# Whole-tile transposes of q and k, and a full-height last matmul, in an attention and feed-forward kernel

## Chip, cores, metric

One core of one Trainium2 chip. The metric is the device time of one execution in microseconds, lower is better.

## What is computed

Three layers one after another on 4 batches of 576 tokens: attention with 8 heads of 64 in a sliding window of 64 tokens, a convolutional gated feed-forward layer, and a second feed-forward layer with a product over the token axis.

```
scores = q @ k.T / 8, kept where 0 <= i - j < 64
x = softmax(scores) @ v                     # per head, then heads side by side: (4, 576, 512)
h = relu(x @ w_in)                          # 1024 wide
c = conv over tokens, 3 taps per channel
y = (h * sigmoid(c)) @ w_out
u, v = split(relu(y @ w2_in)); v = layernorm(v)
v_s = einsum('ts,bsd->btd', w_spatial, v) + b_spatial
out = (u * v_s) @ w2_out
```

The weights w_in, w_out, w2_in and w2_out arrive as 64-bit numbers and are turned into 32-bit ones on the chip.

## The kernel before

Large products run in a reduced 32-bit form on TensorE, with every operand split into a high part and the rest; high x high, high x rest and rest x high are summed in PSUM (`split`, line 288).

Nothing is written out in program order. Each operation is recorded with a rank (a due time), the engines that may run it with an estimated cost for each, and what it reads and writes (`Plan.op`, line 94); `Plan.emit` (line 115) then plays the estimates through and emits, on each engine, the ready operation of the lowest rank. The engines run what is emitted strictly in that order. So a changed cost in an operation can change the order of others. All loads are issued from one queue, SyncE's (SPq in the profile).

*Attention.* Batch 0 has its q and k loaded in five tiles of 128 tokens (the last has 64), by `rec_load_qk` (line 425), and transposed on TensorE by `rec_qk` (line 466): q goes into the block-diagonal tiles qbd, k into kT, by copies out of the PSUM tile tr, of which there is one. In tile 0 the tokens lie on 128 partitions, and four transposes of 128x128 do it (line 478). In tiles 1 to 4, chosen by `pairs` (line 422), two neighbouring tokens share a partition, so that 64 partitions (32 in the last tile) hold rows of 128 numbers; 16 small operations follow, 8 transposes (line 489) and 8 matmuls with the identity (line 487), and the copies put even and odd tokens back in place. The matmuls execute twice each for 32-bit operands, the transposes once. The other batches are transposed on VectorE.

A block of 64 queries is a round (`rec_round`, line 534): scores on TensorE (s, line 543), mask and row maximum on VectorE (line 555), exponential on ScalarE (line 563), reciprocal on VectorE (lines 570, 571), normalising on GpSimd or VectorE (line 575), transposes (pt, line 585), a copy to pts, the product with v (pv, line 598), and the split into x. There are 36 rounds. The PSUM tiles s, pt and pv exist once each.

*First feed-forward.* h (lines 681 to 683) starts when the first five rounds of batch 0 are through and the first slice of w_in is converted. A conversion takes two bit operations and a join on VectorE (lines 387, 393, 399) and a scaled copy on ScalarE, VectorE or GpSimd; its raw load goes into one of two raw tiles. The three taps of the convolution are VectorE work (line 709).

*Second feed-forward.* `rec_sp` (line 1003) computes the product over tokens for one batch, 128 channels and half of the tokens: 14 matmuls into one PSUM tile of 288 columns. The contraction runs over four whole tiles of 128 tokens, three matmuls each (lines 1018 to 1020), and over the last 64 tokens. For these, the tile vtl holds the high part of v on partitions 0 to 63 and the rest on 64 to 127, and the last tile of the spatial weights wspg holds its 64 rows twice. One matmul on 128 rows with the weights' high part gives two of the products (line 1023), one on 64 rows with the weights' rest gives the third:

```
mm(sps(), vv[:, ds], ws[:, 0, o], start=False, stop=False)
mm(sps(), vv[0:TAIL, ds], ws[0:TAIL, 1, o], start=False, stop=True)
```

There are 32 such groups, eight a batch. Behind each follow an add of the bias on VectorE (line 1032), a product with u on GpSimd or VectorE (line 1035), and the split into gd (lines 265 and 286); two gr tiles and two PSUM tiles take turns.

Of the kernel before, what the change touches and what calls it, by code (L numbers as in the profile page):

```python
# [19 lines left out]
# leads, spacings and engine weights of the plan below  # L20
# [45 lines left out]
class Buf:  # L66
    """One tile of a rotating tag, made when its first user is emitted."""
# [14 lines left out]
class Plan:  # L82
    """Orders the emission: each operation has a rank, engines it may run on with estimated
    costs, and the regions and tiles it touches. Recorded in an order that is right when run
    one after another; each engine then takes the ready operation of the lowest rank."""
# [105 lines left out]
def tile_attention_convglu_spatial(  # L191
# [59 lines left out]
    def mk(pool, shape, dt, tag, name, n):  # L251
        """A tile of a tag; `pool` may be a list that holds the pool when the tile is made."""
        return plan.buf(
            tag, n,
            lambda: (pool[0] if isinstance(pool, list) else pool).tile(shape, dt, tag=tag, name=name, bufs=n),
        )
# [31 lines left out]
    def split(rank, n, src, hi, lo, r, w, b, psum=False, hi_engs="AV", lo_engs="V", hi_cost=None):  # L288
        """hi = src to float32r; lo = src - hi, exact."""
        costs = {"A": c_act(n, psum), "V": c_tt(n) if psum else c_ts(n), "P": 0.00238 * n + 0.1}  # L290
        op(rank, {e: costs[e] for e in hi_engs}, lambda e: copy_to(e, hi(), src()), r=r, w=[(w, "h")], b=b)
        lc = {"V": c_tt(n), "P": 0.00238 * n + 0.1}
        op(
            rank + 0.01, {e: lc[e] for e in lo_engs}, lambda e: sub_to(e, lo(), src(), hi()),
            r=list(r) + [(w, "h")], w=[(w, "l")], b=b,
        )
# [84 lines left out]
    def halves(x_):  # L381
        """The 16-bit halves of 32-bit words, the low one first."""
        return x_.bitcast(H16).rearrange("p (c w) -> p c w", w=2)

    def low_bits(u, raw):
        """The upper three bits of the low words, as the lowest bits of u."""
        nc.vector.tensor_scalar(
            out=halves(u)[:, :, 0], in0=halves(raw.rearrange("p c w -> p (c w)"))[:, 0::2, 1],
            scalar1=13, scalar2=None, op0=ALU.logical_shift_right,
        )  # L390
# [31 lines left out]
    def pairs(t):  # L422
        return 30 >> t & 1

    def rec_load_qk(b, t, rank):
        """Batch 0: rows of tokens. Later: tokens in rows of 32, each group of 32 partitions
        with its 32 columns of a head pair."""
        for src, dst, nm in ((q, qn, "qn"), (k, kn, "kn")):
            if b < B0:
                n = min(P, S - t * P)  # L430
                if pairs(t):
                    a = mk(at, [W, H, 2 * D], F, nm, nm, 2)
                else:
                    a = mk(at, [P, H, D], F, nm, nm, 2)

                def ld(e, a=a, src=src, n=n):
                    if pairs(t):
                        nc.sync.dma_start(
                            out=a()[:n // 2], in_=src[b, :, t * P:t * P + n, :].rearrange("h (p r) d -> p h (r d)", r=2)
                        )  # L440
                    else:
                        nc.sync.dma_start(out=a()[:n], in_=src[b, :, t * P:t * P + n, :].rearrange("h p d -> p h d"))
                op(rank, {"D": (0.73 if pairs(t) else 1.46) * n / P}, ld, w=[(nm, b, t)], b=[a])
            else:
                a = mk(at, [P, HP, 2 * UB, 32], F, nm, nm, 2)
                n = UB * W
                for g in range(4):
                    def ld(e, a=a, src=src, g=g):
                        for hp in range(HP):
                            part = src[b, 2 * hp + g // 2, t * n:(t + 1) * n, 32 * (g % 2):32 * (g % 2) + 32]  # L450
                            nc.sync.dma_start(
                                out=a()[32 * g:32 * g + 32, hp], in_=part.rearrange("(u t) c -> t u c", t=32)
                            )
                    op(rank + 0.01 * g, {"D": 1.9}, ld, w=[(nm, b, t, g)], b=[a])
            dst[b, t] = a
# [10 lines left out]
    def rec_qk(b, t, rank):  # L466
# [3 lines left out]
        for nm, src in (("q", qn), ("k", kn)):  # L470
            a = src[b, t]
            two = pairs(t)
            pt_ = ps("y" if (b, t, nm) == (0, 0, "k") else "tr", [P, HP, 2, W] if two else [P, HP, P], "tr")

            def tr(e, a=a, pt_=pt_):
                for hp in range(HP):
                    if not two:
                        nc.tensor.transpose(
                            pt_()[:, hp, :n], a()[:n, 2 * hp:2 * hp + 2, :].rearrange("p h d -> p (h d)"), ident[:n, :n]
                        )  # L480
                        continue
                    for h in range(2):
                        for r_ in range(2):
                            o_ = pt_()[h * W:h * W + W, hp, r_, :n // 2]
                            i_ = a()[:n // 2, 2 * hp + h, r_ * D:r_ * D + D]
                            if h:
                                mm(o_, i_, ident[:n // 2, :n // 2], start=True, stop=True)
                            else:
                                nc.tensor.transpose(o_, i_, ident[:n // 2, :n // 2])

            def put(e, dst, rows, c0, m, pt_=pt_):
                if two:
                    copy_to(
                        e, dst.rearrange("p k (c r) -> p k r c", r=2), pt_()[rows, :, :, c0 // 2:(c0 + m) // 2]
                    )
                else:
                    copy_to(e, dst, pt_()[rows, :, c0:c0 + m])
            key = (nm, "tr", b, t)
            op(rank, {"T": HP * (0.32 if two else 0.112)}, tr, r=[(nm + "n", b, t), "ident"], w=[key], b=[a, pt_])
# [111 lines left out]
    def rec_conv(rank, src, view, n, dst=None, b=(), lead=PLAN["LD"]):  # L611
        """float64 words to float32; returns the tile and the key."""
# [164 lines left out]
    # the rounds, in order  # L777
# [186 lines left out]
    # transposed spatial weights: tiles of s on partitions; the last one holds its rows twice  # L964
# [38 lines left out]
    def rec_sp(b, d, c, rank):  # L1003
# [9 lines left out]
        def g(e):  # L1013
            for s in range(NT):
# [6 lines left out]
                else:  # L1021
                    vv = vtl[pp][bj]()
                    mm(sps(), vv[:, ds], ws[:, 0, o], start=False, stop=False)
                    mm(sps(), vv[0:TAIL, ds], ws[0:TAIL, 1, o], start=False, stop=True)  # L1024
# [139 lines left out]
```

## Time and profile before

| | |
|---|---|
| runs (3) | 584.22 us median, 584.21 to 586.52 |
| span of the profiled execution | 582.7 us, 11237 instructions |
| TensorE (PE) busy | 552.4 us, 95%, 4070 matmuls |
| VectorE (DVE) busy | 379.5 us, 65% |
| ScalarE (ACT) busy | 304.3 us, 52% |
| GpSimd (POOL) busy | 177.5 us, 30% |
| mean granted clock of TensorE | 0.967 |
| moved by DMA | 49.71 MB, mean 85 GB/s |

The span runs from the first to the last instruction; a run's time holds some 1.5 us more. A mean busy share hides that stages have different limits, so the views are read stage by stage. In the profile's rows L12 is line 12 of the kernel; the granted clock is a share of 2.4 GHz; PEld is the load of the stationary operand, which overlaps PE; the end of a matmul is modelled, so the distance between two starts says more than the duration of one.

### The profile page before, as it was taken

To read this page: it belongs to the slowest core of one execution; us is meant where nothing else is said; L and a number is where in the kernel's file an instruction comes from. 1 tells how busy PE (TensorE), PEld (TensorE's weight loads), DVE (VectorE), ACT (ScalarE), POOL (GpSimd) and SP (SyncE) were. 2 spreads that over 40 slices of the span, in tenths; PEclk is the share of its full clock that TensorE was granted. 3 is DMA by queue.
4 is the path that set the end of the run, shared out by engine and by line. 5 is a ranking of instruction groups with operands and counts; after the bars stand their busy time and mean duration, and the time that the engine had idled before them with its cause. 6 is when DMAs were issued, how large, how long until landed. Compare 5 with 4: busy or idle time off the path is not lost.

```text
span 582.7 us, 11237 instructions
## 1 busy us (share of the span) xinstructions
PE 552.4 (95%) x4070; PEld 504.0 (86%) x4070; DVE 379.5 (65%) x1021; ACT 304.3 (52%) x829; POOL 177.5 (30%) x163
## 2 busy tenths in 40 slices
PE   7999768899999999999999669999999999999997
PEld 6779657899999999999999669898898889888986
DVE  3469999876978587577559991997515661562050
ACT  4557645876866776677675642662322332233222
POOL 2547563440432423223325360024113100310130
PEclk9569989999999999999999888999999999999999
DMA  9647354345244344353136733320012011001002
GB/s 194 169 127 187 102 139 91 64 93 111 53 96 98 66 98 87 59 105 75 39 109 206 217 100 130 80 100 1 37 38 81 1 54 37 1 1 73 1 1 90
DMA packets 119418, 49.71 MB, mean 85 GB/s; under 512 B 99820, under 2 KB 111876, under 8 KB 119364
## 3 DMA queue, kind: packets, MB, share of 16 engines
q1 hardware_dynamic: 119364, 49.01, 33.4%
q8 instruction: 32, 0.52, 0.4%
q14 instruction: 22, 0.18, 0.1%
HBM read 39.54 MB, written 9.44 MB: 84 GB/s over the span
## 4 chain that ended last, share of the span: by engine, by line
PE 76%; DVE 16%; DMA 4%; ACT 2%; issue 2%; POOL 0%; SPq 0%; DVEq 0%; POOLq 0%; ACTq 0%
PE s L543 5%; DVE cv L709 5%; PE y L749 4%; PE y L748 4%; PE y L750 4%; PE sps L1018 4%; PE h L681 4%; PE h L682 3%; PE h L683 3%; PE vps L893 3%; PE sps L1020 3%; PE sps L1019 3%; PE ops L1071 3%; PE vps L894 3%; PE ops L1072 3%; PE vps L895 3%
## 5 line engine op out<-in xcount | busy, mean ns | idle before, releaser
L709 DVE SCALAR_TENSOR_TENSOR cv<-hs,cw,cv 128x288 f32<-128x288 f32 x128 | 86.5, 687 | 24.1 <-ACT cv L704 22.9
L681 PE MATMUL h<-x,wi 128*128 128x290 f32 x256 | 79.9, 312 | 11.1 <-ACT hs L281 8.3
L748 PE MATMUL y<-g,wo 128*128 128x288 f32 x256 | 80.7, 315 | 5.0 <-ACT g L265 2.8
L750 PE MATMUL y<-g,wo 128*128 128x288 f32 x256 | 77.4, 302 | 0.8 <-POOL wo L286 0.8
L749 PE MATMUL y<-g,wo 128*128 128x288 f32 x256 | 77.8, 304 | 0.2 <-DVE g L286 0.2
L682 PE MATMUL h<-x,wi 128*128 128x290 f32 x256 | 76.8, 300 | 0.5 <-DVE x L286 0.5
L683 PE MATMUL h<-x,wi 128*128 128x290 f32 x256 | 76.6, 299 | 0.0
L286 POOL TENSOR_TENSOR g<-cv,g 128x576 fp32r<-128x576 f32 x31 | 47.0, 1517 | 80.9 <-ACT g L265 79.4
L575 POOL TENSOR_TENSOR sm<-sm,st 128x512 f32<-128x512 f32 x36 | 39.5, 1098 | 71.2 <-DVE st L571 46.9
L681 PEld LDWEIGHTS h<-x,wi 128*128 128x128 f32 x256 | 49.1, 192 | 12.9 <-ACT hs L281 9.6
L563 ACT ACTIVATE sm<-sm,st 128x128 f32<-128x128 f32 x144 | 55.9, 390 | 8.1 <-DVE st L555 8.0
L748 PEld LDWEIGHTS y<-g,wo 128*128 128x128 f32 x256 | 49.9, 195 | 6.4 <-ACT g L265 3.0
L750 PEld LDWEIGHTS y<-g,wo 128*128 128x128 f32 x256 | 49.8, 195 | 1.1 <-POOL wo L286 1.1
L749 PEld LDWEIGHTS y<-g,wo 128*128 128x128 f32 x256 | 50.1, 196 | 0.5 <-DVE g L286 0.5
L682 PEld LDWEIGHTS h<-x,wi 128*128 128x128 f32 x256 | 49.2, 192 | 0.7 <-DVE x L286 0.7
L683 PEld LDWEIGHTS h<-x,wi 128*128 128x128 f32 x256 | 49.2, 192 | 0.0
L1035 POOL TENSOR_TENSOR gr<-gr,ut 128x288 f32<-128x288 f32 x30 | 25.4, 847 | 77.5 <-DVE gr L1032 74.7
L543 PE MATMUL s<-kT,qbd 128*128 128x128 f32 x288 | 42.8, 295 | 1.7 <-DVE kT L522 1.2
L1032 DVE TENSOR_TENSOR gr<-sps,bb 128x288 f32<-128x288 f32 x32 | 14.6, 456 | 44.9 <-PE sps L1024 44.8
L265 ACT ACTIVATE gd<-gr 128x288 fp32r<-128x288 f32 (+1 forms) x32 | 13.4, 417 | 56.3 <-POOL gr L1035 51.4
L555 DVE CUSTOM_DVE_ANT_0 sm<-s,mask_n 128x128 f32<-128x128 f32 x128 | 29.4, 285 | 19.2 <-PE s L543 19.1
L543 PEld LDWEIGHTS s<-kT,qbd 128*128 128x128 f32 x288 | 37.8, 203 | 3.6 <-DVE kT L522 1.6
(176 smaller groups left out, 1452.0 us busy)
## 6 DMA issues: line engine op xcount, KB each, us to landing
raw<-in_moe_w_in_dram SPq DMA_DIRECT2D x16, 512.0 KB, 4.9
vw<-in_v_dram SPq DMA_DIRECT2D x32, 256.0 KB, 3.8
raw<-in_moe_w_out_dram SPq DMA_DIRECT2D x12, 512.0 KB, 3.6
yd<-ys SPq DMA_DIRECT2D x32, 144.0 KB, 1.8
yr<-yd SPq DMA_DIRECT2D x16, 288.0 KB, 4.0
out_dram<-osb SPq DMA_DIRECT2D x15, 256.0 KB, 2.0
qn<-in_q_dram SPq DMA_DIRECT2D x144, 24.0 KB, 2.0
kn<-in_k_dram SPq DMA_DIRECT2D x144, 24.0 KB, 2.0
```

What stands on the lines that cost most here:

```text
L286: (nc.gpsimd if e == "P" else nc.vector).tensor_tensor(out=out_, in0=a, in1=b.bitcast(F), op=ALU.subtract)
L543: mm(pss()[:, hp, :], qbd[j][:, hp, :], kT[:, hp, k0 * W:k0 * W + P], start=True, stop=True,)
L555: nc.vector.tensor_tensor_reduce(out=sm()[:, hp, :], in0=pss()[:, hp, :], in1=mask, scale=-scale, scalar=BIG, op0=ALU.add, op1=ALU.min, ac ...
L563: nc.scalar.activation(out=sm()[:, hp, :], in_=sm()[:, hp, :], func=ACTF.Exp, scale=-1.0, bias=st()[:, 0, hp:hp + 1], accum_out=st()[:, 1, ...
L575: (nc.gpsimd if e == "P" else nc.vector).tensor_tensor(out=sm(), in0=sm(), in1=st()[:, 2, :].unsqueeze(2).to_broadcast([P, HP, P]), op=ALU ...
L681: mm(hps(), wh, xh, start=(kk == 0), stop=False)
L682: mm(hps(), wh, xl, start=False, stop=False)
L683: mm(hps(), wl, xh, start=False, stop=(kk == KD - 1))
L709: return lambda e: nc.vector.scalar_tensor_tensor(out=cv(), in0=h[:, o + j:o + j + CH], scalar=cw[:, j, f:f + 1], in1=cv(), op0=ALU.mult, ...
L748: mm(yps(), wt[:, 0], gt[:, 0, :], start=(kk == 0), stop=False)
L749: mm(yps(), wt[:, 0], gt[:, 1, :], start=False, stop=False)
L750: mm(yps(), wt[:, 1], gt[:, 0, :], start=False, stop=(kk == KF - 1))
```

## The change

Batch 0's tiles 1 to 4 of q and k are loaded and transposed as tile 0 is. The planner is told of longer loads (1.46 instead of 0.73 for 128 tokens) and shorter transposes (4 x 0.112 instead of 4 x 0.32). In the product over tokens the last matmul uses all 128 rows of vtl and of the weights' rest, which adds rest x rest, a product that was left out before. Comments are dropped too.

```diff
-    def pairs(t):
-        return 30 >> t & 1
...
                 n = min(P, S - t * P)
-                if pairs(t):
-                    a = mk(at, [W, H, 2 * D], F, nm, nm, 2)
-                else:
-                    a = mk(at, [P, H, D], F, nm, nm, 2)
+                a = mk(at, [P, H, D], F, nm, nm, 2)
 
                 def ld(e, a=a, src=src, n=n):
-                    if pairs(t):
-                        nc.sync.dma_start(
-                            out=a()[:n // 2], in_=src[b, :, t * P:t * P + n, :].rearrange("h (p r) d -> p h (r d)", r=2)
-                        )
-                    else:
-                        nc.sync.dma_start(out=a()[:n], in_=src[b, :, t * P:t * P + n, :].rearrange("h p d -> p h d"))
-                op(rank, {"D": (0.73 if pairs(t) else 1.46) * n / P}, ld, w=[(nm, b, t)], b=[a])
+                    nc.sync.dma_start(out=a()[:n], in_=src[b, :, t * P:t * P + n, :].rearrange("h p d -> p h d"))
+                op(rank, {"D": 1.46 * n / P}, ld, w=[(nm, b, t)], b=[a])
...
                 for hp in range(HP):
-                    if not two:
-                        nc.tensor.transpose(
-                            pt_()[:, hp, :n], a()[:n, 2 * hp:2 * hp + 2, :].rearrange("p h d -> p (h d)"), ident[:n, :n]
-                        )
-                        continue
-                    for h in range(2):
-                        for r_ in range(2):
-                            o_ = pt_()[h * W:h * W + W, hp, r_, :n // 2]
-                            i_ = a()[:n // 2, 2 * hp + h, r_ * D:r_ * D + D]
-                            if h:
-                                mm(o_, i_, ident[:n // 2, :n // 2], start=True, stop=True)
-                            else:
-                                nc.tensor.transpose(o_, i_, ident[:n // 2, :n // 2])
+                    nc.tensor.transpose(
+                        pt_()[:, hp, :n], a()[:n, 2 * hp:2 * hp + 2, :].rearrange("p h d -> p (h d)"), ident[:n, :n]
+                    )
 
             def put(e, dst, rows, c0, m, pt_=pt_):
-                if two:
-                    copy_to(
-                        e, dst.rearrange("p k (c r) -> p k r c", r=2), pt_()[rows, :, :, c0 // 2:(c0 + m) // 2]
-                    )
-                else:
-                    copy_to(e, dst, pt_()[rows, :, c0:c0 + m])
+                copy_to(e, dst, pt_()[rows, :, c0:c0 + m])
...
-            op(rank, {"T": HP * (0.32 if two else 0.112)}, tr, r=[(nm + "n", b, t), "ident"], w=[key], b=[a, pt_])
+            op(rank, {"T": HP * 0.112}, tr, r=[(nm + "n", b, t), "ident"], w=[key], b=[a, pt_])
...
                     mm(sps(), vv[:, ds], ws[:, 0, o], start=False, stop=False)
-                    mm(sps(), vv[0:TAIL, ds], ws[0:TAIL, 1, o], start=False, stop=True)
+                    mm(sps(), vv[:, ds], ws[:, 1, o], start=False, stop=True)
```

TensorE's order at the head of the program, before the change (tr is the PSUM tile of the transposes, qn and kn the loaded tiles of q and k, s the scores; the two rows of small operations come four times in a set):

```order
L478 MATMUL tr<-ident,qn 128x128 x4
L478 MATMUL tr<-ident,kn 128x128 x4
L489 MATMUL tr<-ident,qn 64x64 x2
L487 MATMUL tr<-ident,qn 64x64 x2
...
L543 MATMUL s<-kT,qbd_90 128x128 x4
L413 MATMUL cwp<-ident,cwf 128x24
L489 MATMUL tr<-ident,kn 64x64 x2
L487 MATMUL tr<-ident,kn 64x64 x2
...
L543 MATMUL s<-kT,qbd_91 128x128 x4
```

And with the change (lines are those of the changed kernel):

```order
L465 MATMUL tr<-ident,qn 128x128 x4
L465 MATMUL tr<-ident,kn 128x128 x4
L516 MATMUL s<-kT,qbd_90 128x128 x4
L465 MATMUL tr<-ident,qn 128x128 x4
L413 MATMUL cwp<-ident,cwf 128x24
L516 MATMUL s<-kT,qbd_91 128x128 x4
L465 MATMUL tr<-ident,kn 128x128 x4
L516 MATMUL s<-kT,qbd_92 128x128 x4
```

The scores of the first block now stand ahead of the transposes of tile 1 of q, and those of the second ahead of tile 1 of k.

SyncE's loads from the third load of w_in on (raw), before:

```order
L619 DMA raw<-in_moe_w_in_dram 128x4x256
L438 DMA qn<-in_q_dram 64x8x128
L438 DMA kn<-in_k_dram 64x8x128
L619 DMA raw<-in_moe_w_in_dram 128x4x256
L438 DMA qn<-in_q_dram 32x8x128
L438 DMA kn<-in_k_dram 32x8x128
```

And with the change:

```order
L592 DMA raw<-in_moe_w_in_dram 128x4x256
L431 DMA qn<-in_q_dram 128x8x64
L431 DMA kn<-in_k_dram 128x8x64
L451 DMA vw<-in_v_dram 128x8x64
L592 DMA raw<-in_moe_w_in_dram 128x4x256
L451 DMA vw<-in_v_dram 128x8x64
L592 DMA raw<-in_moe_w_in_dram 128x4x256
L431 DMA qn<-in_q_dram 64x8x64
L431 DMA kn<-in_k_dram 64x8x64
```

Two loads of v and the fifth of w_in now stand ahead of the last tile of q and k; a load of v stands ahead of the fourth of w_in.

## Rows read from the trace of the kernel before

**Rows 1.** Stretches: us, busy us of PE, PEld, DVE, ACT, POOL, then clock, DMA, GB/s

```profile
0.00:8.00 8.00, 5.57 (x32) 5.33 (x32) 2.73 (x9) 2.88 (x6) 2.50 (x21) 1.00 0.74 160
...
16.00:39.00 23.00, 23.00 (x144) 17.64 (x142) 12.69 (x55) 11.89 (x43) 9.51 (x9) 0.50 0.45 116
...
0.00:45.00 45.00, 41.95 (x301) 33.67 (x302) 22.33 (x91) 23.03 (x77) 18.40 (x35) 0.73 0.69 164
45.00:117.00 72.00, 57.91 (x508) 52.62 (x509) 69.68 (x152) 47.13 (x131) 39.89 (x31) 0.98 0.47 116
...
300.00:365.00 65.00, 55.65 (x371) 53.09 (x368) 48.47 (x69) 32.39 (x67) 25.27 (x16) 0.92 0.56 168
365.00:583.00 218.00, 214.50 (x1246) 188.45 (x1244) 107.73 (x274) 73.50 (x176) 37.23 (x38) 1.00 0.12 40
```

**Rows 2.** The chain of waits, 0 to 110 us: start, us, what

```profile
44.81 0.29 DVE sm L555
```

**Rows 3.** Timeline of TensorE in the product over tokens: start, us, what

```profile
399.01 0.29 PE L1023 MATMUL sps<-wspg,vtl 128*128 128x288 f32 x1
399.23 0.40 PE L1024 MATMUL sps<-wspg,vtl 64*128 64x288 f32 x1
399.56 0.40 PE L1018 MATMUL sps<-wsp,vn 128*128 128x288 f32 x1
399.79 0.30 PE L1019 MATMUL sps<-wsp,vn 128*128 128x288 f32 x1
...
401.26 0.29 PE L1023 MATMUL sps<-wspg,vtl 128*128 128x288 f32 x1
...
549.39 0.40 PE L1024 MATMUL sps<-wspg,vtl 64*128 64x288 f32 x1
...
565.10 0.40 PE L1024 MATMUL sps<-wspg,vtl 64*128 64x288 f32 x1
```

**Rows 4.** Waits over the whole span: who for whom, us in total, times, longest

```profile
DVE gr L1032 <- PE sps L1024: 44.8, 25, 20.3
```

**Rows 5.** Stretch 0 to 53 us, instructions on tile tr alone: PE, PEld, ACT

```profile
0.00:53.00 53.00, 24.71 (x200) 17.94 (x200) 10.00 (x23) 0.77 0.67 160
```

**Rows 6.** Timeline of TensorE in the head

```profile
5.89 0.60 PE L478 MATMUL tr<-ident,qn 128*128 128x128 f32 x4
6.33 0.60 PE L478 MATMUL tr<-ident,kn 128*128 128x128 f32 x4
8.17 0.30 PE L489 MATMUL tr<-ident,qn 64*64 64x64 f32 x2 [1.24 <-ACT qbd L265]
...
10.57 1.16 PE L543 MATMUL s<-kT,qbd 128*128 128x128 f32 x8
...
16.15 0.42 PE L489 MATMUL tr<-ident,qn 64*64 64x64 f32 x2
...
19.99 2.07 PE L543 MATMUL s<-kT,qbd 128*128 128x128 f32 x8
...
26.69 2.07 PE L543 MATMUL s<-kT,qbd 128*128 128x128 f32 x8
...
29.75 1.12 PE L585 MATMUL pt<-ident,sm 128*128 128x128 f32 x4
...
53.08 0.38 PE L681 MATMUL h<-x,wi 128*128 128x290 f32 x1
```

**Rows 7.** Waits of VectorE, 0 to 53 us

```profile
DVE sm L555 <- PE s L543: 14.2, 7, 3.2
DVE wu L387 <- DMA raw<-in_moe_w_in_dram: 3.2, 1, 3.2
```

**Rows 8.** Waits of TensorE, 318 to 372 us

```profile
PE h L681 <- ACT hs L281: 3.2, 1, 3.2
```

**Rows 9.** From issue to landing: first the loads of tile 0 (L442), then tiles 1 to 4

```profile
DMA to landing us min/median/max: 3.4/3.9/4.4
DMA to landing us min/median/max: 2.2/5.4/7.6
```

More of the change, by code (lines that the diff above doesn't have):

```diff
@@ L471, in rec_qk @@
             a = src[b, t]
-            two = pairs(t)
-            pt_ = ps("y" if (b, t, nm) == (0, 0, "k") else "tr", [P, HP, 2, W] if two else [P, HP, P], "tr")
+            pt_ = ps("y" if (b, t, nm) == (0, 0, "k") else "tr", [P, HP, P], "tr")
             def tr(e, a=a, pt_=pt_):
                 for hp in range(HP):
-                    if not two:
-                        nc.tensor.transpose(
-                            pt_()[:, hp, :n], a()[:n, 2 * hp:2 * hp + 2, :].rearrange("p h d -> p (h d)"), ident[:n, :n]
-                        )
-                        continue
-                    for h in range(2):
-                        for r_ in range(2):
-                            o_ = pt_()[h * W:h * W + W, hp, r_, :n // 2]
-                            i_ = a()[:n // 2, 2 * hp + h, r_ * D:r_ * D + D]
-                            if h:
-                                mm(o_, i_, ident[:n // 2, :n // 2], start=True, stop=True)
-                            else:
-                                nc.tensor.transpose(o_, i_, ident[:n // 2, :n // 2])
-            def put(e, dst, rows, c0, m, pt_=pt_):
-                if two:
-                    copy_to(
-                        e, dst.rearrange("p k (c r) -> p k r c", r=2), pt_()[rows, :, :, c0 // 2:(c0 + m) // 2]
-                    )
-                else:
-                    copy_to(e, dst, pt_()[rows, :, c0:c0 + m])
+                    nc.tensor.transpose(
+                        pt_()[:, hp, :n], a()[:n, 2 * hp:2 * hp + 2, :].rearrange("p h d -> p (h d)"), ident[:n, :n]
+                    )
+            def put(e, dst, rows, c0, m, pt_=pt_):
+                copy_to(e, dst, pt_()[rows, :, c0:c0 + m])
             key = (nm, "tr", b, t)
-            op(rank, {"T": HP * (0.32 if two else 0.112)}, tr, r=[(nm + "n", b, t), "ident"], w=[key], b=[a, pt_])
+            op(rank, {"T": HP * 0.112}, tr, r=[(nm + "n", b, t), "ident"], w=[key], b=[a, pt_])
             if nm == "q":
```

## Prediction

> **What bounds the kernel now.** I read the stretches first, then the chain of waits, then the timeline of TensorE at the two places that the diff touches.
>
> The stretches [rows 1] show three regimes. Up to 45 us TensorE is busy for 41.95 of 45 us, at a mean granted clock of 0.73, while VectorE does only 22.33 us of work. From 45 to 117 us VectorE is busy for 69.68 of 72 us and TensorE for 57.91. Later TensorE is the bound, with 214.50 of the 218 us from 365 to the end; between, from 300 to 365 us, is a looser place (55.65 of 65 us), where the second set of weights arrives.
>
> The chain [rows 2] agrees: TensorE's transposes and scores lead it up to 44.81 us, where VectorE takes over. So a shorter TensorE job in the head can count only as far as it lets VectorE begin its 92 us of work (22.33 + 69.68) earlier. A shorter one in the spatial product, inside the last stretch, counts in full.
>
> **Term 1, the spatial product.** It runs 32 groups of 14 matmuls. Around the one on 64 rows (L1024) the starts stand apart [rows 3]: 0.22 us from L1023 to L1024, 0.33 us to the next group's L1018, 0.23 us to L1019; the 11 steps from there to the group's L1023 (399.79 to 401.26) take 0.134 us each. No wait stands in these gaps; what differs is the form, from 128 rows to 64 and back. The change makes that matmul one on 128 rows like L1023, on tiles that L1023 or its neighbours already read, so no load, copy or wait is added. Seven groups now take 565.10 - 549.39 = 15.71 us, 2.244 each. At the plain distance a group takes 14 x 0.1336 = 1.870 us. The gain is 0.374 us a group, over 32 groups **12.0 us**. All of them lie in the TensorE-bound stretch. I allow 0.5 us each way for the reading of the distances (0.015 us a group).
>
> What could take it back is the work behind each group, which two gr tiles and two PSUM tiles hand on. VectorE, which begins it, waited for TensorE's last matmul in 25 of the 32 groups, 44.8 us in total [rows 4], so it has room for groups that come 0.37 us sooner (12 us in all). If it had not, TensorE would wait in its place and the gain would end with that cover; I book nothing.
>
> **Term 2, the head.** For tiles 1 to 4 of q and of k the old kernel runs 16 small operations, of which eight execute twice. All work on the tile tr takes 24.71 us of TensorE [rows 5]; tile 0's two sets are 0.60 each, so the eight changed sets hold 23.5 us: 2.40 for the first (8.17 to 10.57), 3.84 for one at half clock (16.15 to 19.99) [rows 6]. The new form is that of tile 0, four transposes: 0.44 us at the full clock (5.89 to 6.33), and at half clock 1.12, which four transposes of the same size take in L585 [rows 6]. The granted clock was 0.50, its 1.2 GHz level, from 16 to 39 us [rows 1], where four of the sets begin. So the new sets take about 4 x 0.44 + 4 x 1.12 = 6.2 us, and TensorE loses **17.3 us** of work from its path.
>
> What is late next? On TensorE at half clock a round would still need scores 2.07, pt 1.12, pv about as much and one set 1.12, 5.4 us; now the scores of two rounds stand 6.7 us apart (19.99, 26.69) [rows 6]. ScalarE has 23.03 us of work in these 45 us [rows 1], as much as VectorE, so TensorE stays the head's limit at half clock, and the other two share it at full clock.
>
> The gain at 117 us is the VectorE idle time that goes. Now it is 45 - 22.33 = 22.7 us. Some stays: in the first 8 us VectorE has 2.73 us of setting up [rows 1], and the first scores can start near 8.8 us (10.57 less most of the set of tile 1, which stood ahead of them: the head's order, above), so that nothing comes before 9.9 us: 9.9 - 2.7 = 7.2 us idle. At most 22.7 - 7.2 = 15.5 us can go. For the lower end: 14.2 us of the idle time are seven waits for scores [rows 7], six of them after the first round, and each shrinks by the round's 6.7 - 5.4 = 1.3 us or more: 7.8 us. I take **10 us**, nearer to the lower end, because the rows of the head that it is nearest to are at half clock. The outer ends, 0 and the whole 17.3, are rivals below.
>
> **Edits that I book at nothing.** Copies out of PSUM no longer interleave pairs; they move as many elements, on ScalarE, beside TensorE's work. If they were slower, the next scores would wait for them. The planner, told of other costs, gives other orders. On SyncE a load of v now stands ahead of the fourth load of w_in, and two of v and one of w_in ahead of the last tile of q and k; the two raw tiles cover the first, and the last tile is wanted only two rounds later. In the loose place from 300 to 365 us a changed order can gain or lose a wait; the longest of TensorE there is 3.2 us [rows 8], so I keep 3 us each way.
>
> The loads of tiles 1 to 4 fetch 256-byte pieces where they fetched 512. Tile 0 has that form already: 256 KB landed in 3.4 and 4.4 us, against 2.2 to 7.6 us, median 5.4, for the 512-byte form, which met a fuller queue [rows 9]. I book nothing. The Trainium skill (DMA: Bandwidth & Descriptors, Specifications) speaks against the change: it asks for at least 512 B per transfer for line rate and says that smaller ones cost a read-modify-write. By that rule the eight changed loads would be slower; these rows, of loads into SBUF, do not bear it out, and what it would cost is rival B.
>
> **Sum.** The profiled execution has a span of 582.7 us; the median of the runs is 584.2, so about 1.5 us lie around the span, and they stay. 584.2 - 12.0 - 10 = 562.2, say **562 us**. The case's own range: 584.2 - 12.5 - 15.5 - 3 = 553 to 584.2 - 11.5 - 7.8 + 3 = 568.
>
> **The rivals.**
> A. *The head's saving stays hidden.* VectorE's idle time in the head is set by the weights, which come through two raw tiles, and by a round's own chain through four engines, so the VectorE-bound stretch ends at 117 us as before. For it speaks that the chain from 44.81 us on is VectorE's [rows 2]; against it that VectorE's waits in the head were for scores, 14.2 us, and only 3.2 us for a load of weights [rows 7]. Time 584.2 - 12.0 = 572.2. Chance 0.17.
> B. *256-byte pieces are slow.* As a mechanism of this kernel: q and k of tiles 2 and 3 land in twice the time, some 7 us later than now (7.6 us at most [rows 9]), while the new head wants them no later than the old. Then rounds 4 to 7 wait for loads and some 6 of the 10 us are lost: 568. Tile 0's loads speak against it. Chance 0.10.
> C. *All of it passes through.* The full clock returns earlier than 39 us and VectorE fills its gaps with conversions: 584.2 - 12.0 - 17.3 = 554.9. Chance 0.12.
> D. *Slower, by the clock.* TensorE has less to do in the head, and the level of 1.2 GHz, now left at 39 us, lasts into the VectorE-bound stretch. That stretch holds 57.91 us of TensorE work in 72 us [rows 1]. Each microsecond of it done at half clock takes one more; 14 us are slack and 22 us are what the change gains, so the kernel is slower once 36 us of that work run at half clock, which is when the low level lasts to about 90 us. If it lasted to 117 us: 584.2 - 22 + (58 - 14) = 606. Against it: over that stretch, with TensorE busy for eight tenths, the mean granted clock was 0.98 [rows 1]. Chance 0.03.
>
> **How the numbers follow.** The forecast has the remaining 0.58. The range 552 to 573 reaches from C, with 3 us of order, to A. A measurement of this kernel can tell about 0.5% (2.9 us) from no change. All cases but D lie beyond that; of A's chance I leave 0.02 for an order that loses another 10 us and more, which ends as no change: faster 0.95, same 0.02, slower 0.03.
>
> **What would show it.** Term 1: the last matmul of a group (now L997) on 128 rows, its neighbours 0.13 us away, a group every 1.87 us, and the part after 365 us shorter by 12. Term 2: sets of four transposes of 0.44 or 1.12 us; the first h matmul, now at 53.08 us [rows 6], some 10 to 17 us earlier; the VectorE-bound stretch ending near 107 us. A is shown by an early first h and a VectorE stretch that still ends near 117; B by loads of tiles 2 and 3 that land more than 8 us after their issue, with TensorE waiting for them; D by a granted clock of 0.5 beyond 60 us. The forecast is wrong if a group of the spatial product stays above 2 us, or the time lies outside 553 to 568.

## The result, and the profile after

The changed kernel takes 569.89 us (median of 4 runs, 568.38 to 571.46); the kernel before, beside it, 585.37 (4 runs, 584.21 to 588.05). The ratio is 0.973, with a 95% interval of 0.969 to 0.977. The span of the profiled execution falls from 582.7 to 566.5 us. That is 16.2 us, of the 22 forecast. Executions of the kernel before spread from 576 us at a mean granted clock of 0.98 to 588 at 0.95 (one took 682, at 0.74); the ratios leave out those more than 1.5% above its fastest in the same set of runs, so they can lie nearer to 1 than the quotient of two medians.

The stretches of the changed kernel, with the columns of [rows 1]; the last two answer to nothing there:

```profile
0.00:45.00 45.00, 31.52 (x296) 27.77 (x297) 34.68 (x121) 34.94 (x113) 23.81 (x39) 1.00 0.83 196
45.00:117.00 72.00, 56.23 (x426) 53.25 (x425) 65.98 (x141) 43.45 (x113) 34.99 (x27) 0.83 0.43 107
16.00:39.00 23.00, 16.60 (x189) 14.16 (x190) 21.01 (x72) 20.02 (x67) 15.35 (x13) 1.00 0.72 186
300.00:365.00 65.00, 55.30 (x336) 51.08 (x336) 49.91 (x85) 31.27 (x69) 22.54 (x14) 0.89 0.49 151
365.00:583.00 218.00, 196.41 (x1219) 181.06 (x1217) 101.28 (x254) 69.04 (x164) 37.59 (x38) 1.00 0.11 38
60.00:70.00 10.00, 1.87 (x15) 1.63 (x13) 9.93 (x21) 5.39 (x16) 6.98 (x6) 0.78 0.46 129
70.00:117.00 47.00, 43.07 (x326) 40.87 (x327) 41.19 (x102) 29.35 (x79) 19.10 (x15) 0.87 0.43 99
```

In the head, the first 45 us, TensorE is busy for 10.4 us less and VectorE gets 12.4 us more done (34.68 against 22.33). From 16 to 39 us the granted clock is now 1.00, the level of 2.4 GHz, with TensorE busy for 16.60 of 23 us; before, it was busy all the 23 us at 0.50. Behind the head there is a hole: from 60 to 70 us TensorE works for 1.87 us, while VectorE is full, and from 70 to 117 us VectorE has 5.8 us idle. The waits of TensorE from 0 to 117 us and its timeline (start, us, what, idle time before and its releaser) name the hole:

```profile
PE pt L558 <- POOL sm L548: 12.3, 4, 8.6
PE pv L571 <- issue: 3.7, 1, 3.7
```

```profile
61.58 0.29 PE L656 MATMUL h<-x,wi 128*128 128x290 f32 x1
70.49 1.12 PE L558 MATMUL pt<-ident,sm 128*128 128x128 f32 x4 [8.62 <-POOL sm L548]
71.26 0.59 PE L721 MATMUL y<-g,wo 128*128 128x288 f32 x1
71.65 0.44 PE L722 MATMUL y<-g,wo 128*128 128x288 f32 x1
71.89 0.44 PE L723 MATMUL y<-g,wo 128*128 128x288 f32 x1
```

The transposes that wait are those of batch 0's ninth round (round 8, counted from 0). Behind the wait, matmuls start 0.24 us apart, not 0.13: the low clock again (0.54 granted from 70 to 80 us).

How far the change is ahead of or behind the kernel before, along the program, is read from the start of the same matmul in TensorE's timelines of both (us, negative where ahead; sps is the PSUM tile of the spatial product; the end is the last start of an output matmul). All are differences to one execution of the kernel before, the one of 582.7 us. The other columns belong to the experiments below.

| place | change | e1 (spatial alone) | e2 (head alone) | e3 (old costs) | e6 (round 8 earlier) |
|---|---|---|---|---|---|
| first h matmul (53.1 before) | -16.4 | +3.5 | -15.9 | -9.4 | -14.3 |
| 97th h (82.9) | -2.5 | +1.7 | -2.0 | -10.9 | -14.3 |
| first y (77.0) | -5.8 | +1.7 | -5.2 | -10.9 | +2.5 |
| 673rd h (302.0) | -7.0 | +2.0 | -6.4 | -11.0 | -1.6 |
| first sps, batch 0 (390.2) | -5.9 | +1.1 | -5.3 | -11.8 | -5.0 |
| first sps, batch 1 (437.2) | -7.0 | -0.3 | -4.0 | -13.3 | -6.2 |
| first sps, batch 2 (495.1) | -10.0 | -3.3 | -4.0 | -16.3 | -9.2 |
| first sps, batch 3 (547.6) | -13.1 | -6.3 | -4.0 | -19.3 | -12.3 |
| end (579.2) | -16.2 | -9.5 | -4.0 | -22.5 | -15.5 |

So the head gives 16.4 us at the first h matmul, 7.0 of which are left in the first feed-forward, and the spatial product gives 10.3 us: about 3.0 in each of batches 1 to 3, but only 1.1 in batch 0. In that batch TensorE waits once for a PSUM tile; before there was no such wait. TensorE's and VectorE's timelines there:

```profile
387.72 0.29 PE L996 MATMUL sps<-wspg,vtl 128*128 128x288 f32 x1
387.85 0.29 PE L997 MATMUL sps<-wspg,vtl 128*128 128x288 f32 x1
390.00 0.40 PE L991 MATMUL sps<-wsp,vn 128*128 128x288 f32 x1 [1.85 <-DVE gr L1005]
```

```profile
386.96 1.05 DVE L886 SCALAR_TENSOR_TENSOR lst<-lst 128x1 f32<-128x1 f32 x1
388.04 0.15 DVE L889 TENSOR_SCALAR lst<-lst 128x1 f32<-128x1 f32 x1
388.23 0.16 DVE L890 RECIPROCAL lst<-lst 128x1 f32<-128x1 f32 x1
388.43 0.55 DVE L891 TENSOR_SCALAR vf<-vr,lst 128x512 f32<-128x512 f32 x1
388.90 0.68 DVE L286 TENSOR_TENSOR ytl<-ytr,ytl 128x512 fp32r<-128x512 f32 x1
389.50 0.81 DVE L1005 TENSOR_TENSOR gr<-sps,bb 128x288 f32<-128x288 f32 x2
```

The second group ends at 388.1, and no third can start until the first group's bias add has read its PSUM tile. That add stands on VectorE behind the layer norm of a v tile of batch 1 and a split of y. By contrast the form of the matmul is as forecast (instruction, count, ns min/median/max), and 0.13 us lie between it and its neighbours:

```profile
L997 PE MATMUL sps<-wspg,vtl x32: 291/294/297, 386.0 to 549.2; 128*128 128x288 f32 x32
```

And the loads of q and k of batch 0, ten in 256-byte pieces now, landed no later on the whole than the eight 512-byte ones of [rows 9]:

```profile
DMA to landing us min/median/max: 3.3/4.5/5.9
```

Only the two 128 KB loads of the last tile took longer: 4.4 us for q and 3.9 for k, against 3.7 and 2.2.

### The profile page after: what moved, and what is told of

It is laid out like the page before. It is cut to its first block, busy times and chain, and to the rows that moved or that the text cites. A ratio compares the mean times of both kernels' runs of the same rounds, so it can differ in the third digit from the quotient of the medians.

```text
span 566.5 us, 10918 instructions
## 1 busy us (share of the span) xinstructions
PE 521.2 (92%) x3910; PEld 488.7 (86%) x3910; DVE 384.5 (68%) x1019; ACT 305.2 (54%) x832; POOL 174.8 (31%) x162
## 4 chain that ended last, share of the span: by engine, by line
PE 66%; DVE 23%; issue 4%; ACT 4%; DMA 2%; SPq 1%; POOL 0%; DVEq 0%; ACTq 0%; POOLq 0%
DVE cv L682 5%; PE y L722 4%; PE y L721 4%; PE y L723 4%; PE s L516 4%; PE h L654 4%; PE h L655 4%; PE h L656 4%; DVE wu L393 3%; PE ops L1045 3%; PE ops L1044 3%; PE sps L991 3%; PE ops L1046 3%; PE sps L993 3%; PE sps L992 3%
## 5 line engine op out<-in xcount | busy, mean ns | idle before, releaser
L682 DVE SCALAR_TENSOR_TENSOR cv<-hs,cw,cv 128x288 f32<-128x288 f32 x128 | 86.9, 688 | 18.9 <-ACT cv L677 17.7
L721 PE MATMUL y<-g,wo 128*128 128x288 f32 x256 | 82.0, 320 | 3.8 <-ACT ys L265 3.8
L722 PE MATMUL y<-g,wo 128*128 128x288 f32 x256 | 79.0, 309 | 1.0 <-DVE g L286 1.0
L723 PE MATMUL y<-g,wo 128*128 128x288 f32 x256 | 78.6, 307 | 0.4 <-POOL wo L286 0.4
L721 PEld LDWEIGHTS y<-g,wo 128*128 128x128 f32 x256 | 50.9, 199 | 4.9 <-ACT ys L265 4.3
L722 PEld LDWEIGHTS y<-g,wo 128*128 128x128 f32 x256 | 51.2, 200 | 1.3 <-DVE g L286 1.3
L655 PEld LDWEIGHTS h<-x,wi 128*128 128x128 f32 x256 | 49.8, 194 | 2.8 <-DVE x L286 2.8
L654 PEld LDWEIGHTS h<-x,wi 128*128 128x128 f32 x256 | 49.8, 194 | 2.3 <-ACT x L265 1.3
L723 PEld LDWEIGHTS y<-g,wo 128*128 128x128 f32 x256 | 50.9, 199 | 0.7 <-POOL wo L286 0.7
L656 PEld LDWEIGHTS h<-x,wi 128*128 128x128 f32 x256 | 49.7, 194 | 0.0
L516 PE MATMUL s<-kT,qbd 128*128 128x128 f32 x288 | 40.2, 284 | 5.2 <-ACT kT L265 3.5
L516 PEld LDWEIGHTS s<-kT,qbd 128*128 128x128 f32 x288 | 36.1, 195 | 7.2 <-ACT kT L265 4.2
L927 PE MATMUL ups<-yt,w2i 128*128 128x288 f32 x128 | 38.1, 298 | 3.4 <-DVE w2i L270 3.4
L281 ACT ACTIVATE hs<-h 128x290 f32<-128x290 f32 x63 | 25.3, 406 | 28.5 <-PE h L656 28.2
```

The lines of the kernel that those rows point to most:

```text
L516: mm(pss()[:, hp, :], qbd[j][:, hp, :], kT[:, hp, k0 * W:k0 * W + P], start=True, stop=True,)
L654: mm(hps(), wh, xh, start=(kk == 0), stop=False)
L655: mm(hps(), wh, xl, start=False, stop=False)
L656: mm(hps(), wl, xh, start=False, stop=(kk == KD - 1))
L682: return lambda e: nc.vector.scalar_tensor_tensor(out=cv(), in0=h[:, o + j:o + j + CH], scalar=cw[:, j, f:f + 1], in1=cv(), op0=ALU.mult, ...
L721: mm(yps(), wt[:, 0], gt[:, 0, :], start=(kk == 0), stop=False)
```

## The experiments

Two theories for the 9 us of the head's gain that are gone by the 673rd h matmul. **Theory 1**: the planner's order. Told of cheaper transposes and dearer loads, it now issues the first 24 h matmuls ahead of the transposes of k's last tile, and 72 ahead of round 8's scores; round 8 is late, and the second chunk of h, from the 97th matmul on, needs its x. **Theory 2**: VectorE, full from 45 us on, takes the gain back whatever the order.

Because the kernel before varies so, the changed kernels are compared with each other where they can be. e1 to e4 ran on one chip, e5 to e8 on a second, e9 to e11 on a third and e12 on a fourth; the chip of the first result is not on record. The two kernels that were run twice differ in their medians by 0.9 us (the change and e5) and 1.4 us (e3 and e10).

### e1: the spatial product alone

```diff
 (kernel before)
-mm(sps(), vv[0:TAIL, ds], ws[0:TAIL, 1, o], start=False, stop=True)
+mm(sps(), vv[:, ds], ws[:, 1, o], start=False, stop=True)
```

> Only the last matmul of each group of the spatial product goes to 128 rows; the order on every engine stays that of the kernel before. Both theories expect the head unchanged (first h matmul near 53 us) and 32 x 0.374 = 12.0 us less: a ratio near 0.980, 572 us against 584. If the first batch's groups are covered badly, as in the changed kernel, where nothing was gained between its 48th vps matmul and its first ops matmul, 3 us of it are missing: 575 us.

Measured: 574.38 us (573.74 to 576.01); ratio 0.987 (0.979 to 0.995). The table gives 10.6 us from the first spatial matmul to the end: 1.4, 3.0, 3.0, 3.2 by batch. In the first, the waits of TensorE from 391 to 414 us are

```profile
PE sps L1018 <- DVE gr L1032: 0.8, 2, 0.6
```

The 3.0 us of the later batches are the forecast's 8 x 0.374. The first batch alone falls short, with no change in the head to blame; the wait shown is 0.8 of the 1.6 us that it lacks.

### e2: the head alone

```diff
 (changed kernel)
-mm(sps(), vv[:, ds], ws[:, 1, o], start=False, stop=True)
+mm(sps(), vv[0:TAIL, ds], ws[0:TAIL, 1, o], start=False, stop=True)
```

> The change without its spatial part; order as in the changed kernel. If the two parts add up: about 569.9 + 9 to 12 = 579 to 582 us, a ratio of 0.990 to 0.995, with the first h matmul near 37 us and a wait of 8 to 9 us of TensorE for the normalised scores of the ninth round near 62 to 70 us, as in the changed kernel.

Measured: 582.08 us (579.84 to 582.98); ratio 1.000 (0.995 to 1.005). So the runs show no gain of the head alone, in the planner's new order; the gains below are those of the profiled executions. The trace repeats the changed kernel's head, with the wait of 8.9 us in it:

```profile
PE pt L558 <- POOL sm L548: 12.6, 4, 8.9
```

It is 6.4 us ahead at the 673rd h matmul, and 4.0 at the end. The two parts, -9.5 and -4.0, make -13.5 of the -16.2. The difference is e1's head, 1.1 us late by the first spatial matmul, the head of e2, 0.6 us behind that of the change, and the first batch, where e2 falls back by 1.3 us and e1 gains 1.4, while the change gains 1.1. e2's 1.3 us are a wait for the first bias add, with the old form of the matmul (383 to 435 us):

```profile
PE sps L991 <- DVE gr L1005: 1.3, 1, 1.3
```

In the new order TensorE runs the first batch's eight groups one behind the other; in the kernel before, a v tile's 12 matmuls stand between the second and the third. So the order brings most of that wait by itself, and from e2 to the change, in one order, the form gives 2.4 us in the first batch and 11.6 from the first spatial matmul to the end.

### e3 and e10: the new transposes, the old order

```diff
 (changed kernel)
-op(rank, {"D": 1.46 * n / P}, ld, ...)
+op(rank, {"D": (0.73 if t else 1.46) * n / P}, ld, ...)
...
-op(rank, {"T": HP * 0.112}, tr, ...)
+op(rank, {"T": HP * (0.32 if t else 0.112)}, tr, ...)
```

The operations are those of the change; the planner is told the old costs, and so emits the order of the kernel before. With the order goes the choice of engines: about a dozen operations run on another engine than in the change, among them three scaled copies of raw weights on VectorE that the change has on ScalarE. Both are meant by "order" below.

> The whole change, but the planner is told the old costs of tiles 1 to 4, so that the order on all engines is that of the kernel before. Theory 1 (the head's saving is given back by the new order, which puts the ninth round's transposes ahead of products that are ready): no wait of 8.6 us, TensorE's clock stays up after 45 us, and the time is 4 to 9 us below the changed kernel, 561 to 566 us. Theory 2 (VectorE is saturated from 35 to 105 us and takes back whatever the head gains beyond some 7 us, in any order): within 2 us of the changed kernel, 568 to 572 us.

> The kernel with the old planner costs once more, on the chip of the other two runs, as their mark. Theory 1 and theory 2 both: 560 to 563 us, steady offset -10 to -11 us.

Measured: 561.06 us (560.17 to 562.05), ratio 0.964 (0.956 to 0.972); on another chip 562.41 (560.94 to 563.13), ratio 0.968 (0.963 to 0.974). The changed kernel's two medians, the second on a third chip, are 569.89 and 570.80 (e5): 7.5 to 9.7 us more, and no run of the one overlaps with one of the other. The wait of round 8's transposes is gone (0.4 us left), and the lead of 10.9 us at the 97th h matmul is kept to the end of the layer. The stretches, as above:

```profile
0.00:45.00 45.00, 34.54 (x247) 29.78 (x248) 34.71 (x132) 30.26 (x103) 27.10 (x42) 0.81 0.87 204
45.00:117.00 72.00, 60.96 (x498) 56.56 (x498) 68.04 (x154) 47.44 (x134) 35.28 (x26) 0.95 0.43 106
70.00:117.00 47.00, 41.34 (x318) 39.13 (x319) 43.86 (x119) 32.40 (x96) 19.26 (x15) 0.93 0.41 92
```

VectorE's share of the head is the same as in the change, 34.7 us. From 70 to 117 us it has 3.1 us idle in place of 5.8. The order is worth 7.5 to 9.7 us, and theory 2, as "whatever the order", falls.

### e4: the old cost of the loads alone

```diff
 (changed kernel)
-op(rank, {"D": 1.46 * n / P}, ld, ...)
+op(rank, {"D": (0.73 if t else 1.46) * n / P}, ld, ...)
```

> The whole change, but only the load's cost is told to the planner as before; the transposes' is the new one. All transposes and all scores of batch 0 then stand ahead of the first h matmul. Theory 1: first h later than 37 us by 2 to 4 us, no wait of TensorE over 4 us behind the ninth round, 561 to 567 us. Theory 2: 568 to 572 us.

Measured: 566.53 us (565.73 to 567.12), ratio 0.973 (0.963 to 0.982), 3.4 to 4.3 us less than the change. Round 8 moves ahead of the first h matmul and the 97th h comes 17.3 us early; but TensorE then waits 7.3 us in one piece for a k transpose of VectorE (kT), and at the first y matmul it is 0.9 us behind the kernel before. The hole has moved.

### e5: the changed kernel again, as a mark

> The changed kernel once more, on the chip of the three runs below, as their mark. Both theories: 567 to 571 us; first h matmul near 36.7 us, the wait of round 8's transposes for the normalised scores near 8.6 us, steady offset to before near -7 us.

Measured: 570.80 us (569.21 to 574.58), as expected, with the wait of 8.9 us. The kernel before, beside it, took 578.03 us (576.03 to 583.93) here, so the ratio is 0.987 (0.979 to 0.994): a gain of 7 us by the medians, where the first runs showed 15. Which part of the program the kernel before is faster in then, no trace shows. The lead of e5 at the 673rd h matmul is 4.7 us in the profiled execution.

### e6: round 8 earlier

```diff
 (changed kernel; m == 8 is tile 4, or round 8)
-rec_round(b, i, t_round[m])
+rec_round(b, i, t_round[m] - (14.0 if m == 8 else 0.0))
```

The ranks of tile 4's load and transposes move likewise.

> The changed kernel with the load, the transposes and the whole of round 8 (the last of batch 0) ranked 14 units of the plan earlier: k tile 4's transposes now stand ahead of the first h matmul and round 8's scores behind 36 of them, not 72. Theory 1 (the late chain of round 8 is what gives back the head's gain): the 8.6 us wait falls under 3 us, the 97th h matmul comes at least 8 us earlier than in the kernel before (the change alone: 2.5), and the time falls by 3 to 6 us to 562 to 566. Theory 2 (VectorE sets the pace from 45 to 110 us whatever the order): the wait moves to another place, the offset at the 192nd h matmul stays between -5 and -8 us, and the time stays within 568 to 571.

Measured: 568.83 us (567.42 to 570.45), 2.0 less than e5, with ranges that overlap. The waits of TensorE from 30 to 130 us, the first five lines:

```profile
PE h L654 <- ACT hs L281: 4.6, 3, 3.4
PE pv L571 <- ACT sm L536: 3.7, 1, 3.7
PE pv L571 <- ACT pts L265: 3.0, 2, 2.0
PE s L516 <- DVE st L528: 2.9, 1, 2.9
PE pt L558 <- POOL sm L548: 2.4, 3, 0.9
```

The long wait goes and the 97th h matmul is 14.3 us early, as theory 1 wanted; but the lead is spent by the first y (+2.5), in waits for other chains. That is theory 2's pattern, and its time. The lateness of round 8 alone is not what the order costs.

### e7: filler in the wait

```diff
 (changed kernel, transposes of a round)
 def tr(e):
+    if (b, i) == (0, 8):
+        for _ in range(64):
+            nc.tensor.transpose(psp()[:, 0, :], ident, ident)
```

> The changed kernel with 64 extra transposes of the identity (0.11 us each at full clock, 7 us in all) put on TensorE just ahead of round 8's four transposes, into the same tile, so that TensorE works through its wait of 8.6 us and nothing else moves. Clock theory (the fall to half clock behind that wait costs time): granted clock from 66 to 86 us at 0.9 or more instead of 0.54 to 0.83, the h matmuls near 84 us at 0.12 instead of 0.24 us apart, and the time 2 to 4 us shorter, 564 to 567. Without a price on the clock (VectorE sets the pace there anyway): the clock rises but the time stays within 1 us of the changed kernel.

Measured: 570.06 us (569.32 to 571.01) beside 570.80 for e5, with ranges that overlap. From 60 to 80 us the clock stood at 1.00 (0.66 in the changed kernel), and VectorE did the same 19.09 us of work in both:

```profile
60.00:80.00 20.00, 14.05 (x120) 12.89 (x120) 19.09 (x33) 9.62 (x25) 12.27 (x10) 1.00 0.48 130
80.00:90.00 10.00, 7.64 (x40) 7.32 (x41) 8.69 (x16) 5.34 (x11) 4.08 (x3) 0.66 0.63 141
```

From 80 to 90 us the clock is lower instead, 0.66 against 0.83, so the filler put the low level off and did not remove it. What the run shows is that the full clock in the 20 us behind the hole's start gives under 1 us by the medians: TensorE is not the bound there.

### e8: one of VectorE's conversion steps twice

```diff
 (e3)
-low_bits(u(), raw())
+for _ in range(2 if rank < 200 else 1):
+    low_bits(u(), raw())
```

> The kernel with the old planner costs (561 us), with the low-bits instruction of the 16 weight conversions of the first phase done twice on VectorE (about 0.46 us each undisturbed, 0.67 us mean where they ran from 20 to 80 us: 7 to 11 us of VectorE work), PE's order unchanged. Theory 2 (VectorE, busy 99% from 40 to 90 us there, sets the pace): 5 to 10 us longer, 566 to 571, with the offset there from the first y matmul on. Theory 1 alone (only TensorE's order decides): under 1.5 us longer, 560 to 563.

Measured: 569.79 us (568.72 to 570.48), 8.7 more than e3 and 7.4 more than e10. The line's group from 0 to 120 us (count, busy us, mean ns) was 16 instructions and 11.2 us in e3:

```profile
L387 DVE TENSOR_SCALAR wu<-raw 128x512 uint16<-128x512 uint16 x32 | 26.2, 818 | 4.2 <-DMA raw<-in_moe_w_in_dram 3.6
```

That is 15.0 us more in this line, but the durations of neighbouring instructions overlap, and others became shorter (L399 13.1 us in place of 17.0). VectorE's busy time up to the same point of the program, the end of its 24th instruction of the convolution (L682 in e3), says what was really put on; first e3, then e8:

```profile
0.00:95.93 95.93, 75.62 (x559) 67.66 (x560) 84.56 (x213) 60.04 (x176) 53.76 (x61) 0.88 0.64 155
0.00:103.74 103.74, 75.87 (x559) 68.30 (x560) 93.46 (x229) 60.38 (x176) 53.49 (x61) 0.85 0.58 143
```

Of 8.9 us more, or 10.0 beside e10's 83.47, 7.4 to 8.7 come through. TensorE's order is the same, so VectorE is a bound in the old order too.

### e9: two of VectorE's conversion steps as one

```diff
 (changed kernel)
-low_bits(u(), raw())
-sign_bits(u(), raw())
+if rank < 200:
+    nc.vector.tensor_scalar(out=u(), in0=raw()[:, :, 1], scalar1=-2 ** 31, scalar2=None, op0=ALU.bitwise_and)
+    return
+low_bits(u(), raw())
+sign_bits(u(), raw())
```

The 16 weight conversions of the first feed-forward take the mask, which leaves out the lowest three bits of these weights.

> The changed kernel with the low-bits and the sign instruction of the 16 weight conversions of the first phase (717 and 820 ns mean there) replaced by one 32-bit mask; the lowest three bits of those weights are left out. TensorE's order is unchanged. 16 x 1.54 us fall away and 16 x about 0.7 to 1.1 us come, so 7 to 13 us of VectorE work go. Theory 2 (VectorE sets the pace of the changed kernel's stretch to 110 us as well): the steady offset deepens by 5 to 10 us and the time falls to 560 to 565. Theory 1 (TensorE's order, with round 8 late, sets it): within 2 us of the changed kernel's 570.8.

Measured: 564.83 us (564.29 to 565.21), 5.1 to 6.0 less than the changed kernel. From 0 to 120 us 11.8 us of VectorE work take the place of 24.6 (11.5 for L387, 13.1 for L393):

```profile
L604 DVE TENSOR_SCALAR wu<-raw 128x512 int32<-128x512 int32 x16 | 11.8, 740 | 0.5 <-DMA raw<-in_moe_w_in_dram 0.5
```

Again the line's sum, 12.8 us less, is more than what was taken off. Up to the end of the same 24th instruction VectorE's busy time is 84.69 us in the change and 76.55 in e9:

```profile
0.00:98.23 98.23, 69.37 (x547) 63.61 (x548) 84.69 (x209) 64.56 (x181) 51.92 (x60) 0.88 0.61 150
0.00:93.17 93.17, 68.71 (x547) 62.09 (x548) 76.55 (x193) 63.70 (x181) 52.63 (x60) 0.91 0.64 158
```

Of 8.1 us less, 5.1 to 6.0 come through, with TensorE's order of the change and its long wait (7.6 us) still there. So both hold: VectorE's work and the order set the time together.

### e11 and e12: the first batch of the spatial product

```diff
 (e11, on e3: low halves of batch 1's normalised tiles)
-[(key, "f")], ("vn", b, m), [vf, dst],
+[(key, "f")], ("vn", b, m), [vf, dst], lo_engs=("P" if b == 1 else "V"),
 (e12, on e3: the plan's cost of the square root)
-op(rank + 4.2, {"A": 0.1}, ...)
+op(rank + 4.2, {"A": 1.0 if b == 1 else 0.1}, ...)
```

> The kernel with the old planner costs, with the low halves of batch 1's normalised tiles made on GpSimd instead of VectorE (some 0.9 us each; three of them run between the first spatial groups), TensorE's order unchanged. If the first batch's spatial stage falls short (1.5 us gained where the later batches gain 3.0) because its bias adds stand behind VectorE's layer-norm work: the sps waits of 0.8 us in all go, the first batch gains 2 to 3 us, and the time is 0.6 to 1.5 us shorter than the run above. If the shortfall has another cause (the u and v groups between, GpSimd's multiply): within 0.3 us of it or longer.

> The kernel with the old planner costs, with ScalarE's square root of batch 1's layer norm booked at 1.0 instead of 0.1 in the plan: VectorE now has the first spatial group's bias add ahead of the last steps of a layer norm instead of behind them, and one v tile's 12 matmuls stand behind six spatial groups instead of ahead. If the queue behind the layer norm is what the first batch lacks: the two sps waits (0.6 the longest) go, the first batch of the spatial product gains 2.5 to 3.0 us against the kernel before (1.5 in the runs with the old costs), and the time falls by 1 to 1.5 us, to 559.5 to 561.5. If other work takes the place (the v tile behind the groups, GpSimd's multiply): no gain in that stage, 561 to 563.

Measured: e11 560.68 us (560.49 to 560.81), e12 563.06 (562.17 to 564.10), beside 562.41 for e10, which ran on e11's chip. The waits of TensorE for the PSUM tile, first e11 (370 to 404 us), then e12 (370 to 408 us):

```profile
PE sps L991 <- DVE gr L1005: 1.1, 3, 0.6
```

```profile
PE sps L991 <- DVE gr L1005: 2.4, 1, 2.4
```

Neither edit takes the wait away. In e11 the low halves are gone from VectorE, but the chain of small layer-norm steps still stands ahead of the first add. In e12 the first add comes early and the second stands behind the same steps. What e11 gains on e10 lies ahead of the spatial product (1.3 us by the 673rd h matmul, 1.3 more by the first spatial matmul), which the edit doesn't explain; in the first batch itself e11 gains 1.3 us on the kernel before and e12 loses 1.0. No run gave the first batch its 3.0 us; an order that keeps all adds clear of the layer norm was not found.

## Why the prediction was right, and where not

The sign was right, and so was the mechanism of both terms. The size was not: 562 was 8 us too low, and 569.89 lies outside the 553 to 568 that the forecast set itself as the sign of being wrong. It lies within the wider 552 to 573 because that reaches to rival A, whose mechanism is not the one that made up the time; in that the range was lucky. Beside the kernel before Term 1 brought 10.3 of 12.0 us and Term 2 about 6 of 10. What was missing is the planner's order in the main, which was booked at nothing, with 3 us each way.

**Term 1.** The reading of the gaps held: the matmul on 128 rows follows its neighbours at 0.13 us, and each later batch gains 3.0 us, which is 8 x 0.374. The Trainium skill (TensorEngine Tiling (Array Packing), Key Properties) says that a change of the tiling mode drains TensorE; if the 64-row form is such a mode, the trace is in line with it, at 0.374 us for the way in and out. The step that failed is "I book nothing" for the work behind each group. I had counted VectorE's waits for the 32 groups together, 44.8 us [rows 4]. By batch, in the kernel before (375 to 437 us, then 437 to 495), the same wait reads

```profile
DVE gr L1032 <- PE sps L1024: 2.6, 3, 1.4
```

```profile
DVE gr L1032 <- PE sps L1024: 6.8, 7, 1.4
```

and 28.5 of the 44.8 us lie behind 547 us, in the last batch. The first has three waits for eight groups, because VectorE also norms batch 1's v tiles there. In the change TensorE waits 1.9 us for it, and 3.0 - 1.9 = 1.1 is what was gained. Of the 1.9, e2 has 1.3 with the old form: that part is the order's. The form adds 0.6 in the new order; in the old one the first batch lacks 1.6 (e1). So the work behind the groups took back 0.4 to 1.4 us of the 12.0: 11.6 were left in the new order, 10.6 in the old.

**Term 2, the head.** Each of the eight sets became four transposes, all at the full clock, which end 0.60 to 0.66 us after the first starts (0.46 in the last tile), as tile 0's do. All work on the tile tr, as in [rows 5]:

```profile
0.00:53.00 53.00, 5.66 (x40) 4.23 (x40) 9.54 (x23) 0.99 0.75 181
```

That is 19 us off TensorE, where 17.3 were forecast. The "4 x 1.12" of that sum, for four sets at half clock, failed: the clock was 1.00 throughout the head. VectorE's idle time there fell by 12.4 us, more than the 10 taken, inside the 7.8 to 15.5, and its waits for scores in the first 53 us fell from 14.2 us to 4.5. The clock need not be the reason: e3 has the same 34.7 us of VectorE work in the head at a granted clock of 0.81. The first h matmul came 16.4 us earlier, inside "10 to 17", but part of that is the order, which moved it ahead of k's last tile: in the old order it came 9.4 (e3) and 10.6 us (e10) earlier. From the 97th to the 673rd h matmul the head is worth 10.2 to 11.0 us in these two, so the 10 was well taken, for that order.

**The planner's order.** This is the step that cost most. I kept 3 us each way, from the longest wait in the loose place near 330 us [rows 8], and looked for its effect there; it was in the head, where the change altered the costs themselves, and it was worth 7.5 to 9.7 us (e3, e10). With both terms in the old order the time is 561.06 and 562.41 us: the 562 is the time of that kernel, not of the changed one. Part of the price can be read off the stretches: VectorE's idle time from 45 to 117 us rose from 2.3 us [rows 1] to 6.0 in the change, against 4.0 in e3, and its instructions became dearer (L393 820 ns in the mean against 703 in e3, L543 544 against 368). 12.4 - 3.7 = 8.7 us of gain would be left by the idle time alone; 7.0 were. This count does not close in every execution (e5 would have 7.3 by it and had 4.7), so it stays a reading. Which piece of the order does it is open: bringing round 8 forward gained 2 us at most (e6), the loads' old cost some 4 (e4).

**The rivals.** A lay nearer than the forecast: 572.2 against 569.9. Its mechanism is partly borne out, since VectorE's work does pass into the time (e8, e9: most of it), but e3 shows that the head's gain need not stay hidden. B falls: 256-byte loads landed in 4.5 us in the median and 5.9 at most, against 5.4 and 7.6, none of them after B's 8 us. The Trainium skill's rule of 512 B (DMA: Bandwidth & Descriptors, Specifications) is about line rate, which no run here tests. Only the two 128 KB loads landed later than before, and they stood at another place in the queue. C did not come. D's sign was there, a clock of 0.54 between 70 and 80 us, but not its price: with the clock held at 1.00 up to 80 us, the time fell by 0.7 us, less than the runs spread (e7).

The best kernels measured are those with the new transposes, the full-height matmul and the planner's old costs: 561.06 and 562.41 us (e3, e10), and 560.68 with e11's edit. They beat both kernels of this case.

## What to carry to other kernels

When a planner's estimate is edited together with the operation it prices, the new order is an edit of its own: run the new operation with the old estimate, and choose by the measured time, not by which estimate is nearer to the truth. A cover must be read where it is needed, batch by batch; a total over the kernel hides the one place that has none. Where two engines are both nearly full, as here, work taken off one or put on it passes into the time for the most part and not in full (5 to 6 of 8 us, 7 to 9 of 9 to 10), and a wait removed in such a stretch can turn up a few microseconds later under another name (e4, e6). What an edit takes off an engine is read from the engine's busy time up to the same point of the program; the durations of one line, summed, overstated it here.

## What was not expected of the hardware

TensorE's clock stood at 0.50 from 16 to 39 us while it was busy for 23.00 of 23 us with 64-row operations, scores and pv, and at 1.00 with 128-row transposes in their place and a busy share of 16.60 of 23. A fuller TensorE was not the one with the higher clock, though a low clock by itself lengthens what counts as busy (four transposes 1.12 us against 0.60, [rows 6]). In e3, the changed kernel's transposes in the other order had 0.75 over that stretch. Nor do the instructions and their order settle it: e1, with the head of the kernel before, was busy for the same 23.00 us at 0.76. What decides between them is open.
